# Relaying the y and z sums per batch on TensorE instead of by DMA copies, in an attention and spectral-mix kernel

## The chip, the cores and the metric

The kernel runs on one core of a Trainium2 chip. The core has five engines, each with its own in-order instruction stream: TensorE (PE in the profile; its weight loads are the row PEld), VectorE (DVE), ScalarE (ACT), GpSimd (POOL) and SyncE (SP, which here issues only transfers). Sixteen DMA engines move data; they are shared by every queue, whichever engine issued the transfer. The metric is the device time of one execution in microseconds (us). Over three runs the kernel before takes 439.65 us in the median (439.11 to 439.7).

## The reference

```python
def phi(x):
    proj = np.einsum('bhsd,df->bhsf', x, w_phi)
    proj = proj - np.max(np.abs(proj), axis=-1, keepdims=True)
    return np.concatenate([np.exp(proj), np.exp(-proj)], axis=-1)
q_p, k_p = (phi(q), phi(k))                    # q, k, v: 8 x 8 x 576 x 64
kv = np.einsum('bhsf,bhsd->bhfd', k_p, v)
z = np.sum(k_p, axis=2)
num = np.einsum('bhsf,bhfd->bhsd', q_p, kv)
den = np.einsum('bhsf,bhf->bhs', q_p, z)[..., None] + 1e-06
x = (num / den), heads side by side             # 8 x 576 x 512
X = np.fft.rfft(x, axis=1)                      # 64 modes are kept
Yr = Xr @ w_r - Xi @ w_i ;  Yi = Xr @ w_i + Xi @ w_r   # w_r, w_i: 64 x 512 x 512, one matrix per mode
y = np.fft.irfft(Y, n=S, axis=1)
u = x + y
return u + np.maximum(u @ w_ch, 0.0)            # w_ch: 512 x 512
```

Inputs and output are float32. The two weight tensors are 67 MB each in float32 and have to be read once.

## The kernel before

**Attention.** The first loop (line 503) runs over 16 units: four groups g of two heads by four pairs bp of batches. Iteration n works on up to four units at different stages: it turns k and q of one, exponentiates and multiplies with v for the next, and takes the finished unit through `freq`, a small matmul with a cosine and sine table that gives its 64 modes. The result x stays in SBUF as `xs`; the modes go to `XT`. Loads of q, k and v are issued by POOL (`load_k`, `load_q`, `load_v`), with a cast to bf16 for q and k; `vn` has two buffers, so the load for unit n + 2 is issued once `weigh_v2` of unit n has read its buffer (the two `va` multiplies on DVE).

**Weights and mix steps.** A mix step (`mix`, line 461) multiplies one load of weights with the modes: 8 modes (one value of o, 0 to 7), one group g of 128 input channels, the real or the imaginary tensor (i = 0 or 1). There are 64 of them, and each needs one load of 1 MB in bf16 (2 MB read as float32 by POOL's queue, which casts). The weights lie in nine rotating buffers of the pool `pw`, tag `wt`; a load waits until the mix step that read its buffer has run, and `next_w(1)` stands after each mix step in the program. The queue is first in, first out. I number the mix steps 0 to 63 in the order in which they run; `some(n)` runs them inside the attention loop, up to number 43, three of these in its last iteration (n = 16). The steps 44 to 63 run in the loop `while mixq` (line 923). The order of the last 20 is: group 3, o = 0 to 5, real and imaginary (44 to 55), then o = 6 and o = 7, each with group 2 real, group 2 imaginary, group 3 real, group 3 imaginary (56 to 63). When the second of a pair of group 3 is done (i = 1), the sums y of these 8 modes are complete: `yst` is 128 rows (8 modes by real and imaginary by 8 batches) of 512.

**What is made of y.** For each o the code adds `yacc` (`yst`, DVE), turns it with four transposes (`yT`), multiplies it with w_ch (8 matmuls, `pz`) into `zst`, and so has y and z = y @ w_ch of these modes. Rows of one o hold all 8 batches, but the inverse transform needs, for one batch, the modes of all o under each other. For that `put` (line 816) sends `yst` and `zst` by DMA from SP into `yall` and `zall`, 128 KB each, in the layout [mode rows, batch, 512]. The rows of o = 6 and 7 go also, as extra copies, into `yl`, four transfers from POOL (o = 6) and four from SP (o = 7).

**Products.** x consists of 36 chunks of 128 tokens by 512: (bp, n) with n = 0 to 8. `Channels.turn` and `product` turn a chunk and multiply it with w_ch: 4 transposes and 4 matmuls, copied by ACT into `xw`. Three chunks (the last of 36, K = 33) are not copied: `hold` leaves their product in PSUM and the z part is added there later.

**Sums.** `Absorb` adds to each chunk the inverse transform of o = 0 to 5 (of o = 0 to 6 for the eight chunks with bp = 0, n < 8, called early): one matmul with `yall` into p (`sum_p`), one with `zall` into q (`sum_q`). DVE adds p to x in `xs` (`keep_x`); ACT copies q into `xw` (`keep_w`). So that the old `xw` is in the sum, a third matmul with the identity adds it first, except for 14 chunks marked `aside`: there ACT copies q into a spare float32 tile and POOL adds `xw`. The order is fixed by the list `todo`: products first, then the sums, taken off by `fill(n)` between the mix steps, with n worked out from what is left.

**PSUM.** In this phase there are eight banks: four single ones (`bank`, tile `pt`) and two double ones (`banks`, tile `pp`). `all` takes alternately two single banks and one double one for p and q.

**Output.** After mix step 63 the part of o = 7 is still missing (o = 6 and 7 for the chunks that aren't early). Lines 984 to 1022 (class `Last`) add it from `yl` or straight from `yst` and `zst`, apply the maximum, add, and store from SP in 20 transfers. The change leaves this part as it is.

Of the kernel before, what the change touches and what calls it, by code (L numbers as in the profile page):

```python
# [19 lines left out]
NG = 4  # L21
# [22 lines left out]
def kernel(  # L44
# [455 lines left out]
    def unit(i):  # L500
        return units[i] if 0 <= i < len(units) else None

    for n in range(-2, len(units) + 1):
        P, Q, K, R = (unit(n + i) for i in (-1, 0, 1, 2))
        X = 0 if n < 4 else 6 if n == 4 else 3
        if Q:
# [4 lines left out]
        if Q:  # L511
            Q.weigh_v2()
            if unit(n + 2):
                unit(n + 2).load_v()
        if P:
# [47 lines left out]
        if Q:  # L563
            Q.num(12)
        some(X - 2 + (n == 12))
        if n == -1:
# [15 lines left out]
    def bank(shape=(128, DMODEL), dt=F32):  # L582
        return pst.tile(list(shape), dt, name="pt", tag="pt")
# [5 lines left out]
    pb = pb_cm.__enter__()  # L589
    xw = pb.tile([128, NP, 9, DMODEL], BF16, name="xw", bufs=1)  # L590
    zall = pw.tile([128, B_, DMODEL], BF16, name="zall", tag="wt")
    yall = pw.tile([128, B_, DMODEL], BF16, name="yall", tag="wt")
# [86 lines left out]
    class Channels:  # L679
# [28 lines left out]

        def hold(self, pf):
            for g in range(NG):  # L710
                pe.matmul(pf, lhsT=self.xT[:, g, :], rhs=wchb[:, g, :],
                          start=(g == 0), stop=False)

    def back(p, c, bp, table, src, r, stop=True, start=False):
# [9 lines left out]
    class Absorb:  # L724
# [34 lines left out]

        def only_x(self):  # L760
            self.sum_p(bank())
            self.keep_x()

        def only_w(self):
            back(self.q, self.n, self.bp, self.table, zall, self.rows)
            self.keep_w()

        def all(self):
            if full.index(self) % 2:
                p, q = bank(), bank()  # L770
            else:
                t = banks()
                p, q = t[:, 0], t[:, 1]
            self.sum_p(p)
            self.sum_q(q)
            self.keep_x()
            self.keep_w()
# [4 lines left out]
    ab = [Absorb(*c) for c in chunks]  # L782
    K = len(ch) - 3
    full = sorted(ab[:K], key=lambda c: c.early)
    spare = []
    for c in full[0:28:2]:
        c.aside = True

    tables = inverse_tables()

    def hold(i):
        next(tables, None)
        if i + 1 < len(ch):
            ch[i + 1].turn()
        if i < K:
            ch[i].product()
            if chunks[i] in stored:
                ch[i].back_x()
            return
        if i == K:  # L800
            t = banks()
            ab[i].q, ab[i + 1].q = t[:, 0], t[:, 1]
        elif i == K + 2:
            ab[i].q = bank()
        ch[i].hold(ab[i].q)

    todo = [ch[0].turn] + [lambda i=i: hold(i) for i in range(len(ch))]
    todo += [c.only_x for c in ab[K:]] + [c.only_w for c in ab[K:]] + [c.all for c in full]
    A = 3 * 3 + K

# [4 lines left out]

    def put(src, o, dst, copies):
        if o < 7:
            sp.dma_start(dst[16 * o:16 * o + 16], src)
        if o > 5:
            for s in copies:  # L820
                r = 32 * s + 16 * (o - 6)
                (pool if o == 6 else sp).dma_start(yl[r:r + 16], src)

# [99 lines left out]
    while mixq:  # L923
# [10 lines left out]
        mix(*key, wts.pop(key), XTb[g % 2], bank)  # L934
        next_w(1)
        left = len(mixq)
        if left > 8:
            n = -(-max(len(todo) - A - 2, 0) // (left - 8))
        elif left == 8:
            n = 2  # L940
        else:
            n = math.ceil(len(todo) / max(left - 0.6, 0.4)) if left else 0
        if g == NG - 1 and i == 1:
# [3 lines left out]
            pt = [bank([128, 2, 128], BF16) for h in range(2)]  # L947
            yT = [pb.tile([128, 2, 128], BF16, name=f"yT{h}") for h in range(2)]
            for h in range(2):
                dve.tensor_tensor(out=yst[:, H * h:H * h + H], in0=py[:, H * h:H * h + H],  # L950
                                  in1=yacc[:, o, H * h:H * h + H], op=ALU.add)
            put(yst, o, yall, (0, 2))
            if o < 5:
                fill(min(n, 1))
            for h in range(2):
                for dc in range(2):
                    pe.transpose(pt[h][:, dc, :],
                                 yst[:, H * h + 128 * dc:H * h + 128 * dc + 128], ident_b)
                if h:
                    dve.tensor_copy(yT[h], pt[h])  # L960
                else:
                    act.copy(yT[h], pt[h])
            if o < 5:
                fill(min(n - 1, 1))
            elif end:
                seq[0].straight(0)
                seq[0].keep_p()
                seq[2].straight(0, (0,))
            cut = (slice(0, 384), slice(384, DMODEL))
            pz = [bank([128, e.stop - e.start]) for e in cut]  # L970
# [8 lines left out]
            dve.tensor_copy(zst[:, cut[1]], pz[1])  # L979
            put(zst, o, zall, (1, 3))  # L980
            fill(max(n - 2, 0) if o < 5 else n)
        else:
# [71 lines left out]
```

## Time and profile before

| what | us |
|---|---|
| median of three runs | 439.65 |
| the profiled execution's own time | 440.25 |
| its span, first to last instruction | 438.5 |
| PE busy, share of the span | 332.0 (76%) |
| DVE busy | 296.4 (68%) |
| ACT busy | 279.4 (64%) |
| POOL busy | 113.0 (26%) |

The profiled execution is 0.60 us slower than the median, and 1.75 us of its time lie outside the span. The page gives the busy time of each engine over the whole span; stages with different limits are averaged in it, so a stage has to be read with the windows and the timeline, which give the same figures for one stretch. Almost every instruction passes through one recording helper, so the profile shows line 37 for all of them, and groups are told apart by the tiles that they write and read: `pt<-wt,XT` is a mix step, `pt<-ident_b,xs` are a chunk's transposes, `pt<-wchb,xT` its product, `xs<-pp,xs` is `keep_x` from a double bank, `rl<-pp` the copy of an `aside` sum. The duration of a matmul in the timeline includes its way through the array, so that successive ones overlap: what one costs in a row of them is the distance from start to start.

### The profile page before, as it was taken

The page shows a single profiled execution, that of the slowest core. Times are in us where ns is not written, and L with a number is a line of the kernel's source. Part 1 is how long each engine was busy: PE and PEld are TensorE (multiplying, and loading weights), DVE is VectorE, ACT ScalarE, POOL GpSimd, SP SyncE. Part 2 cuts the span into 40 slices and gives each one's busy share as a digit, 9 for nine tenths or more (in the row PEclk, how much of TensorE's full clock was granted, in tenths as well). Part 3 has the DMA queues.
Part 4 walks back from the last instruction along what each step waited for, and adds up shares of the span by engine and source line. Part 5 has one row for each costly group of instructions (what it writes and reads, how often), then busy time and mean ns, then how long its engine had stood idle before and what let it go on. Part 6 is the DMA issues. An engine that isn't in the chain of part 4 may idle for free.

```text
span 438.5 us, 10107 instructions
## 1 busy us (share of the span) xinstructions
PE 332.0 (76%) x4190; PEld 202.1 (46%) x4233; DVE 296.4 (68%) x583; ACT 279.4 (64%) x478; POOL 113.0 (26%) x151
## 2 busy tenths in 40 slices
PE   2687678688687687687787787284789999998993
PEld 1355456465465465455465555152444554333320
DVE  5667776765786877976986888243784333886684
ACT  3786786776986886875875876210553442665781
POOL 6232132113221222221222221121101111483072
PEclk9998796789998999996996998876899999999996
DMA  9999999999999999999999999999999999996787
GB/s 213 209 212 210 237 212 237 237 212 248 228 211 239 225 228 232 237 215 235 232 217 239 210 239 211 238 213 212 212 215 223 219 222 224 212 219 135 242 361 309
DMA packets 51710, 99.55 MB, mean 227 GB/s; under 512 B 2512, under 2 KB 13648, under 8 KB 51664
## 3 DMA queue, kind: packets, MB, share of 16 engines
q0 software_dynamic: 45232, 85.86, 99.7%
q1 hardware_dynamic: 6272, 12.98, 8.5%
q8 instruction: 33, 0.54, 0.5%
q14 instruction: 13, 0.11, 0.1%
q10 hardware_dynamic: 160, 0.07, 0.1%
HBM read 163.64 MB, written 9.44 MB: 395 GB/s over the span
## 4 chain that ended last, share of the span: by engine, by line
PE 43%; DVE 22%; ACT 18%; DMA 10%; issue 5%; POOL 0%; POOLq 0%; ACTq 0%; DVEq 0%
PE pt L37 17%; PE one L37 14%; DMA wt<-in_moe_w_r_dram 8%; PE two L37 8%; ACT AB L37 7%; DVE m L37 6%; DVE mk L37 6%; PE pp L37 4%; ACT AQ L37 3%; ACT XT L37 3%; DVE xs L37 2%; DVE XT L37 2%; DMA qb<-in_q_dram 2%; ACT qT L37 1%; DVE yacc L37 1%
## 5 line engine op out<-in xcount | busy, mean ns | idle before, releaser
L37 ACT ACTIVATE AB<-two 128x1024 bf16<-128x1024 f32 x64 | 62.0, 1024 | 10.6 <-DVE mk L37 7.2
L37 ACT ACTIVATE AQ<-two 128x1024 bf16<-128x1024 f32 x64 | 62.6, 1043 | 2.0 <-PE two L37 1.8
L37 ACT CAST xw<-pt 128x512 bf16<-128x512 f32 x50 | 29.4, 588 | 41.9 <-PE pt L37 41.8
L37 DVE TENSOR_REDUCE m<-two 128x8 f32<-128x1024 f32 x32 | 39.2, 1224 | 15.8 <-PE two L37 15.7
L37 DVE TENSOR_TENSOR va<-vn,ee 128x1152 bf16<-128x1152 f32 x32 | 42.0, 1355 | 8.2 <-DMA vn<-in_v_dram 8.2
L37 DVE TENSOR_REDUCE mk<-two 128x8 f32<-128x1024 f32 x32 | 38.9, 1218 | 7.7 <-PE two L37 7.7
L37 POOL DMA_DIRECT2D wt<-in_moe_w_i_dram x28 | 21.0, 750 | 86.4 <-PE pt L37 37.7
L37 POOL DMA_DIRECT2D wt<-in_moe_w_r_dram x30 | 22.5, 751 | 69.2 <-PE one L37 30.7
L37 PE MATMUL pt<-wchb,xT 128*128 128x512 bf16 x127 | 35.6, 393 | 5.2 <-DVE xT L37 3.5
L37 PEld LDWEIGHTS <-xs 128*128 128x128 bf16 x624 | 31.6, 103 | 12.6 <-issue 7.3
L37 PE MATMUL two<-w2blk,qT 128*128 128x256 bf16 x128 | 22.1, 301 | 20.2 <-ACT AB L37 8.4
L37 ACT COPY qT<-one 128x512 bf16<-128x512 bf16 (+1 forms) x32 | 19.3, 641 | 27.5 <-PE one L37 27.2
L37 PEld LDWEIGHTS <-qT 128*128 128x128 bf16 x144 | 14.6, 103 | 36.8 <-issue 33.2
L37 PE MATMUL one<-wt,XT 128*32 128x512 bf16 x304 | 27.5, 452 | 4.9 <-DMA wt<-in_moe_w_i_dram 3.3
L37 PE MATMUL two<-mT,minus 96*128 96x512 bf16 x64 | 28.5, 446 | 3.2 <-issue 1.5
L37 PEld LDWEIGHTS <-AQ 128*128 128x128 bf16 x512 | 25.8, 111 | 8.8 <-issue 5.6
L37 PE MATMUL one<-kvz,AQ 128*128 128x65 bf16 x512 | 28.4, 212 | 1.2 <-ACT qT L37 0.8
L37 DVE COPY xT<-pt 128x512 bf16<-128x512 bf16 x36 | 17.0, 472 | 17.8 <-PE pt L37 17.8
L37 PE MATMUL one<-va,AB 64*128 64x65 bf16 x1024 | 22.5, 199 | 8.3 <-DVE va L37 8.3
L37 DVE RECIPROCAL rd<-one 128x6 f32<-128x6 f32 x48 | 9.4, 196 | 27.6 <-PE one L37 27.5
L37 DVE TENSOR_TENSOR xs<-one,rd 128x384 bf16<-128x384 f32 x48 | 26.7, 557 | 1.6
L37 POOL DMA_DIRECT2D kb<-in_k_dram x16 | 11.4, 714 | 62.2 <-PE one L37 57.2
(151 smaller groups left out, 719.3 us busy)
## 6 DMA issues: line engine op xcount, KB each, us to landing
wt<-in_moe_w_r_dram POOLq DMA_DIRECT2D x30, 1024.0 KB, 28.1
wt<-in_moe_w_i_dram POOLq DMA_DIRECT2D x28, 1024.0 KB, 28.4
out_dram<-of SPq DMA_DIRECT2D x16, 512.0 KB, 4.0
vn<-in_v_dram POOLq DMA_DIRECT2D x14, 576.0 KB, 24.6
kb<-in_k_dram POOLq DMA_DIRECT2D x16, 288.0 KB, 20.4
qb<-in_q_dram POOLq DMA_DIRECT2D x16, 288.0 KB, 18.3
xs<-in_moe_w_i_dram POOLq DMA_DIRECT2D x2, 1024.0 KB, 23.1
vn<-in_v_dram SPq DMA_DIRECT2D x2, 576.0 KB, 4.6
```

What stands on the lines that cost most here:

```text
L37: ins = f(*args, **kwargs)
```

## The change

Seven things change in the phase behind the attention, and two in the attention loop.

- y of o = 0 to 5 is not sent to `yall` and `zall` by DMA any more, and z is not worked out per o. Instead the turned y goes into a new tile `yTa`, [128 channels, 4, batch, o, 16], straight from the transposes' PSUM (two copies per o, by ACT and DVE, with rearranged axes). The tile takes one of the nine weight buffers.
- A new function `relay(b)` makes one batch of `yall` and `zall`: four transposes of `yTa` back into a bank, four matmuls of it with w_ch into a second bank, one copy by DVE (y) and one by ACT (z). There are eight, one per batch. For batches 0 and 1 also o = 6 is in it, which two small DVE copies from `yT` bring into `yTa`.
- o = 6 and 7 keep their own z (8 matmuls) and the copies to `yl`; `put` issues these alone.
- All 36 chunks get a product in `xw` and a sum by `all`; `hold`, `only_x` and `only_w` are gone. The sums are ordered by descending bp.
- `two_banks` hands out the double bank twice and then two single ones, in turn, to sums and relays.
- The list `todo` ends in relay 6, a product, relay 7, the last product, and then the 36 sums with the other six relays between them. All of this stands behind mix step 56.
- `next_w(1)` is left out after three mix steps, as one weight buffer fewer is to be had.
- The attention loop's last iteration runs no mix steps: steps 41 to 43 move into the loop `while mixq`, behind the first products.
- The last unit's v is loaded from SP's queue instead of POOL's.

```diff
@@ -1,4 +1,5 @@
 
+import itertools
 import math
 from contextlib import ExitStack
 
@@ -502,7 +503,7 @@
 
     for n in range(-2, len(units) + 1):
         P, Q, K, R = (unit(n + i) for i in (-1, 0, 1, 2))
-        X = 0 if n < 4 else 6 if n == 4 else 3
+        X = 0 if n < 4 or n == len(units) else 6 if n == 4 else 3
         if Q:
             Q.exp_q(0)
         if K:
@@ -511,7 +512,7 @@
         if Q:
             Q.weigh_v2()
             if unit(n + 2):
-                unit(n + 2).load_v()
+                unit(n + 2).load_v(sp if n + 2 == len(units) - 1 else pool)
         if P:
             P.freq()
             assert not any(key[0] == P.g - 2 for key in mixq)
@@ -562,7 +563,7 @@
                 unit(n + 4).load_q()
         if Q:
             Q.num(12)
-        some(X - 2 + (n == 12))
+        some(X - 2 + (n == 12) if X else 0)
         if n == -1:
             forward_table()
         if n < 3:
@@ -588,6 +589,7 @@
     pb_cm = tc.tile_pool(name="pb", bufs=2)
     pb = pb_cm.__enter__()
     xw = pb.tile([128, NP, 9, DMODEL], BF16, name="xw", bufs=1)
+    yTa = pw.tile([128, 4, B_, 7, 16], BF16, name="yTa", tag="wt")
     zall = pw.tile([128, B_, DMODEL], BF16, name="zall", tag="wt")
     yall = pw.tile([128, B_, DMODEL], BF16, name="yall", tag="wt")
     yl = pw.tile([128, B_, DMODEL], BF16, name="yl", tag="wt")
@@ -706,11 +708,6 @@
                           start=(g == 0), stop=(g == 3))
             act.copy(xw[:, self.bp, self.n, :], pf)
 
-        def hold(self, pf):
-            for g in range(NG):
-                pe.matmul(pf, lhsT=self.xT[:, g, :], rhs=wchb[:, g, :],
-                          start=(g == 0), stop=False)
-
     def back(p, c, bp, table, src, r, stop=True, start=False):
 
         if c < 8:
@@ -757,20 +754,8 @@
             else:
                 act.copy(w, self.q)
 
-        def only_x(self):
-            self.sum_p(bank())
-            self.keep_x()
-
-        def only_w(self):
-            back(self.q, self.n, self.bp, self.table, zall, self.rows)
-            self.keep_w()
-
         def all(self):
-            if full.index(self) % 2:
-                p, q = bank(), bank()
-            else:
-                t = banks()
-                p, q = t[:, 0], t[:, 1]
+            p, q = two_banks()
             self.sum_p(p)
             self.sum_q(q)
             self.keep_x()
@@ -780,46 +765,60 @@
     chunks.sort(key=lambda c: c not in stored)
     ch = [Channels(*c) for c in chunks]
     ab = [Absorb(*c) for c in chunks]
-    K = len(ch) - 3
-    full = sorted(ab[:K], key=lambda c: c.early)
+    full = sorted(ab, key=lambda c: -c.bp)
     spare = []
     for c in full[0:28:2]:
         c.aside = True
+    turn = itertools.cycle((0, 0, 1))
+
+    def two_banks():
+        if next(turn):
+            return bank(), bank()
+        t = banks()
+        return t[:, 0], t[:, 1]
+
+    def relay(b):
+
+        at = slice(0, 6 + (b < 2))
+        n = 16 * at.stop
+        cols = [yTa[:, dc, b, at].rearrange("p o k -> p (o k)") for dc in range(4)]
+        py, pz = two_banks()
+        py = py.bitcast(BF16)[:, 0:512]
+        for dc in range(4):
+            pe.transpose(py[:n, 128 * dc:128 * dc + 128], cols[dc], ident_b)
+        for dc in range(4):
+            pe.matmul(pz[:n], lhsT=cols[dc], rhs=wchb[:, dc, :],
+                      start=(dc == 0), stop=(dc == 3))
+        dve.tensor_copy(yall[:n, b], py[:n])
+        act.copy(zall[:n, b], pz[:n])
 
     tables = inverse_tables()
 
-    def hold(i):
+    def product(i):
         next(tables, None)
         if i + 1 < len(ch):
             ch[i + 1].turn()
-        if i < K:
-            ch[i].product()
-            if chunks[i] in stored:
-                ch[i].back_x()
-            return
-        if i == K:
-            t = banks()
-            ab[i].q, ab[i + 1].q = t[:, 0], t[:, 1]
-        elif i == K + 2:
-            ab[i].q = bank()
-        ch[i].hold(ab[i].q)
-
-    todo = [ch[0].turn] + [lambda i=i: hold(i) for i in range(len(ch))]
-    todo += [c.only_x for c in ab[K:]] + [c.only_w for c in ab[K:]] + [c.all for c in full]
-    A = 3 * 3 + K
+        ch[i].product()
+        if chunks[i] in stored:
+            ch[i].back_x()
+
+    todo = [ch[0].turn] + [lambda i=i: product(i) for i in range(len(ch))]
+    tail = [c.all for c in full]
+    for at, b in ((24, 1), (22, 0), (17, 3), (14, 2), (7, 5), (5, 4)):
+        tail.insert(at, lambda b=b: relay(b))
+    tail = [lambda: relay(6), todo[-2], lambda: relay(7), todo[-1]] + tail
+    A = len(tail)
+    todo[-2:] = tail
 
     def fill(n):
         for _ in range(n):
             if todo:
                 todo.pop(0)()
 
-    def put(src, o, dst, copies):
-        if o < 7:
-            sp.dma_start(dst[16 * o:16 * o + 16], src)
-        if o > 5:
-            for s in copies:
-                r = 32 * s + 16 * (o - 6)
-                (pool if o == 6 else sp).dma_start(yl[r:r + 16], src)
+    def put(src, o, copies):
+        for s in copies:
+            r = 32 * s + 16 * (o - 6)
+            (pool if o == 6 else sp).dma_start(yl[r:r + 16], src)
 
 
     class Last:
@@ -932,8 +931,9 @@
             for c in (seq[0], seq[2]):
                 c.base(0)
         mix(*key, wts.pop(key), XTb[g % 2], bank)
-        next_w(1)
         left = len(mixq)
+        if left not in (19, 9, 8):
+            next_w(1)
         if left > 8:
             n = -(-max(len(todo) - A - 2, 0) // (left - 8))
         elif left == 8:
@@ -945,27 +945,39 @@
             py = pys.pop(o)
             yst = pb.tile([128, DMODEL], BF16, name="yst")
             pt = [bank([128, 2, 128], BF16) for h in range(2)]
-            yT = [pb.tile([128, 2, 128], BF16, name=f"yT{h}") for h in range(2)]
+            yT = [pb.tile([128, 2, 128], BF16, name=f"yT{h}") if o > 5 else None
+                  for h in range(2)]
             for h in range(2):
                 dve.tensor_tensor(out=yst[:, H * h:H * h + H], in0=py[:, H * h:H * h + H],
                                   in1=yacc[:, o, H * h:H * h + H], op=ALU.add)
-            put(yst, o, yall, (0, 2))
-            if o < 5:
+            if o > 5:
+                put(yst, o, (0, 2))
+            if not end:
                 fill(min(n, 1))
             for h in range(2):
                 for dc in range(2):
                     pe.transpose(pt[h][:, dc, :],
                                  yst[:, H * h + 128 * dc:H * h + 128 * dc + 128], ident_b)
+                src = pt[h].rearrange("p c (k b) -> p c b k", b=B_)
+                into = yTa[:, 2 * h:2 * h + 2, :, o] if o < 6 else None
                 if h:
-                    dve.tensor_copy(yT[h], pt[h])
+                    dve.tensor_copy(*((into, src) if o < 6 else (yT[h], pt[h])))
                 else:
-                    act.copy(yT[h], pt[h])
-            if o < 5:
-                fill(min(n - 1, 1))
-            elif end:
+                    act.copy(*((into, src) if o < 6 else (yT[h], pt[h])))
+            if o < 6:
+                fill(n - 1)
+                continue
+            if o == 6:
+                for h in range(2):
+                    dve.tensor_copy(
+                        yTa[:, 2 * h:2 * h + 2, 0:2, 6],
+                        yT[h].rearrange("p c (k b) -> p c b k", b=B_)[:, :, 0:2])
+            if end:
                 seq[0].straight(0)
                 seq[0].keep_p()
                 seq[2].straight(0, (0,))
+            else:
+                fill(1)
             cut = (slice(0, 384), slice(384, DMODEL))
             pz = [bank([128, e.stop - e.start]) for e in cut]
             for e in range(2):
@@ -977,8 +989,8 @@
             zst = pb.tile([128, DMODEL], BF16, name="zst")
             act.copy(zst[:, cut[0]], pz[0])
             dve.tensor_copy(zst[:, cut[1]], pz[1])
-            put(zst, o, zall, (1, 3))
-            fill(max(n - 2, 0) if o < 5 else n)
+            put(zst, o, (1, 3))
+            fill(n - 2)
         else:
             fill(n)
     assert not todo
```

## The prediction

> **What bounds the kernel now.** I read the page's slices first, then the queues in two stretches, then the timeline of PE behind the attention. The slices say that the DMA engines are full until some 40 us before the end:
>
> ```profile
> DMA  9999999999999999999999999999999999996787
> GB/s 213 209 212 210 237 212 237 237 212 248 228 211 239 225 228 232 237 215 235 232 217 239 210 239 211 238 213 212 212 215 223 219 222 224 212 219 135 242 361 309
> ```
>
> The transfers between 280 and 320 us, and then those between 320 and 400 us, show what the copies into `yall` and `zall` cost the stream of weights:
>
> ```profile
> q0 software_dynamic: 4241, 8.45, 111.7%
> ```
>
> ```profile
> q0 software_dynamic: 7790, 15.54, 102.3%
> q1 hardware_dynamic: 2016, 1.84, 8.6%
> ```
>
> POOL's queue (q0) moves 8.45 MB in 40 us alone, but 15.54 MB in 80 us beside the 14 copies of SP's queue (q1, 1.84 MB): 1.36 MB less than twice 8.45, so 6.4 us of stream. Undisturbed, a load of 1.05 MB takes 1.05 / (8.45 / 40) = 4.96 us.
>
> The timeline of PE shows who waits. Steps 43 and 44 wait for weights; the later ones don't. The others are prices:
>
> ```profile
> 297.11 0.66 PE L37 MATMUL one<-wt,XT 128*32 128x512 bf16 x8 [3.30 <-DMA wt<-in_moe_w_i_dram]
> 302.11 1.08 PE L37 MATMUL pt<-wt,XT 128*32 128x512 bf16 x8 [4.34 <-DMA wt<-in_moe_w_r_dram]
> ...
> 351.07 0.66 PE L37 MATMUL pt<-wt,XT 128*32 128x512 bf16 x8
> 351.66 0.40 PE L37 MATMUL pt<-ident_b,xs 128*128 128x128 bf16 x4
> 351.89 1.03 PE L37 MATMUL pt<-wchb,xT 128*128 128x512 bf16 x4
> 352.76 0.39 PE L37 MATMUL pt<-ident_b,xs 128*128 128x128 bf16 x4
> ...
> 368.50 0.66 PE L37 MATMUL pt<-wt,XT 128*32 128x512 bf16 x8
> ...
> 403.11 0.66 PE L37 MATMUL pt<-wt,XT 128*32 128x512 bf16 x8
> ```
>
> From start to start a mix step costs 0.59 us, four transposes 0.23, four matmuls over 512 columns 0.87 (0.217 each). Step 56 starts at 368.50, step 63 at 403.11. The windows between, and from there to the end:
>
> ```profile
> 368.50:403.11 34.61, 32.23 (x192) 12.52 (x193) 25.08 (x42) 21.24 (x39) 19.03 (x19) 1.00 1.04 207
> 403.11:438.50 35.39, 27.62 (x157) 9.24 (x157) 23.12 (x24) 20.16 (x38) 11.38 (x10) 0.90 0.76 283
> ```
>
> PE is busy for 32.2 of 34.6 us (first figure after the length): here PE with the copies behind it is the bound, and the weights are just ahead. The end follows step 63 by 35.39 us of output work.
>
> **The change, part by part.** *Copies gone.* All 14 leave SP's queue and the stream keeps 4.96 us a load. Step 44's weights landed at 302.1; step 56 is twelve loads on, 302.1 + 12 x 4.96 = 361.6; step 63's land at 302.1 + 19 x 4.96 = 396.3. So step 56 may start 368.50 - 361.6 = 6.9 us earlier. The loads' own issue doesn't spoil it: they take 25 to 42 us from issue to landing, five to eight loads deep, and with `yTa` in one buffer a load still waits for the step eight before its own (the last one six before, some 26 us ahead of 396). POOL issues it behind two additions of 1.16 us; the four `yl` transfers of o = 6 follow it on POOL, as now.
>
> *The last v, and three steps moved.* This row is the last unit's v:
>
> ```profile
> 282.33 2.63 DVE L37 TENSOR_TENSOR va<-vn,ee 128x1152 bf16<-128x1152 f32 x2 [8.21 <-DMA vn<-in_v_dram]
> ```
>
> On SP it leaves as soon as its buffer is free (the `va` row of two units before ends at 246.9) and isn't behind five loads. Price on SP: 4.6 us alone at the start, 6.5 for a copy in the full stream, against 24.6 on POOL; any of them is before 274, where DVE wants it. The 8.2 us fall away, but the bytes are the same, and what is late next is the weights of step 41, due at 302.1 - 3 x 4.96 = 287.2. There the products start, 15 us earlier than now. The tables on DVE come along (steps 44 to 48 take 30 us with them, DVE busy 25.6 us of 300 to 340) and end near 317; then a step with two products costs 0.59 + 2 x 1.10 + 0.23 = 3.0 us against 4.96 a load, so PE has caught up with the loads by step 51, at 337, five loads before step 56. Steps 51 to 56 then wait for weights. The two y copies per o (between 0.29 us, `yT`, and 0.73, the `xT` copy with rearranged axes) lie in these waits of 1.9 us; z per o (8 matmuls, 0.87) leaves a stretch that waits anyway, worth nothing. If that cover were gone, 12 x 0.44 = 5 us at most would be DVE's and ACT's, half each.
>
> *Behind step 56.* Relays need o = 5, so they all stand here. PE's content from step 56 to 63, before: 7 steps 4.1, 36 sums (y and z, 0.43 each; the four in halves 0.48) 15.7, 19 identity matmuls 4.1, products and held ones 3.1, o = 6 1.1, the output's first five 1.1: 29.2. The actual 34.61 thus holds 5.4 us of waits. After: the eight relays add 8 x (0.23 + 0.87) = 8.8, three more identities 0.65, the products fall to 2.0: 29.2 + 8.8 + 0.65 - 1.1 = 37.55. The weights for step 63 allow 396.3 - 361.6 = 34.7, so PE remains the bound, not the stream. DVE gets 8 copies more (0.42, the `xT` row), ACT 8 (0.59) and 3: 28 each, of about 42 us.
>
> *The waits.* Removed: at o = 6 PE waited 1.1 us for `yst` and `yT`; now a relay stands between. Step 56, now with 0.9 us of waits, is filled with products and relays, and three sums no longer come in two pieces, where steps 57 and 58 lose 1.2: I count 2.8 us less in all. Added: a double bank is taken again after three users instead of four. These rows tell how long one is held, 388.79 to 390.82:
>
> ```profile
> 388.79 0.39 PE L37 MATMUL pp<-yall,CI 96*128 96x512 bf16 x1
> 389.02 0.38 PE L37 MATMUL pp<-zall,CI 96*128 96x512 bf16 x1
> 389.44 0.69 DVE L37 TENSOR_TENSOR xs<-pp,xs 128x512 bf16<-128x512 f32 x1
> 390.22 0.60 ACT L37 COPY rl<-pp 128x512 f32<-128x512 f32 x1 [0.40 <-DVE xs L37]
> ```
>
> ACT reads only after DVE: 2.0 us, 2.2 with an identity, 2.4 for a relay. Three users give PE 1.5 to 2.3 us of work. Going through the order, six reuses come 0.2 to 0.5 too early, 1.7 in all. PE is in order: what waits for a bank holds back the mix step behind it. Waits after: 5.4 - 2.8 + 1.7 = 4.3. Bounds: 1.5 (six steps with 0.13 us, as the best one now, and the 0.75 for ACT before step 63) and 7.5 (waits in today's share, 5.4 / 29.2 x 37.55 = 6.9, and a third of the reuses). I take 4.3, near the middle and from its own terms.
>
> *Sum.* Step 63 at 361.6 + 37.55 + 4.3 = 403.45, against 403.11. Output unchanged, 35.39: span 438.84, +0.34 us, so 440.59 for the profiled execution, and on the median **440.0**, no change. The stream's 6.9 us are spent on 8.35 us of more PE work, less 1.1 of waits.
>
> *Two rules weighed.* The row has four transposes in 0.23 us. The Trainium skill (TensorE: Matmul & The Clock Gate, Part 4: PE-mode transpose) gives about 275 ns for one in a kernel, which speaks against this change: 32 in the relays would be an estimated 8.8 us instead of 1.8, and the end 447. The row decides.
>
> The clock is the second. Two stretches (the third figure from the end is the granted clock):
>
> ```profile
> 45.60:49.00 3.40, 1.51 (x50) 1.24 (x43) 2.81 (x4) 3.19 (x5) 0.45 (x1) 1.00 1.12 211
> 49.00:52.40 3.40, 2.37 (x17) 1.85 (x17) 2.26 (x7) 2.36 (x9) 0.00 (x0) 0.50 1.12 243
> ```
>
> With PE busy 1.51 of 3.40 us the next stretch runs at half clock. PE's waits of 1.9 us in 4.96 put some stretches near that edge, and 3.4 us at half clock at step 56 would cost 1.7 us. The same page (What's actually happening) asks for a whole idle window of about 3.4 us before the clock falls, which would make it nothing. I take nothing, and put 1.7 in the range.
>
> **Rivals.** *Faster: the relays fill the waits.* For: DVE, at 0.60 us a sum and 25 of 34.6 us, sets the pace of PE's 0.43 to 0.65 now, and relays give it air. Against: the held banks. With waits of 2.0 us step 63 comes at 401.15, the median 437.7.
>
> *Slower: the double banks.* Two of three users now go through two double banks. If one is held 0.4 us longer than above, because DVE or ACT is still at another bank, the early reuses grow from six to about fifteen: 3 us more, 443.0. It decides from 0.1 us of longer holding (0.7 us in all). For: ACT waits for DVE in the row above. Against: relays between sums spread the users out.
>
> *The end belongs to the stream*: PE's work fits into 34.7 us, step 63 at 396.3, median 432.8. Against: 37.55 us are counted.
>
> *The copies cost nothing*, and the stream stays at (8.45 x 2 / 15.54) x 4.96 = 5.39 a load: step 56 at 366.8 as now (its weights), step 63 at 408.65, median 445.2. Against: the two queue rows.
>
> **How the numbers follow.** No change 0.36, relays fill the waits 0.30, double banks or the clock 0.29, stream 0.03, copies 0.02. Of the first, 0.26 lie inside 0.2% (0.9 us, about what a measurement tells from no change), 0.05 on either side: faster 0.38, same 0.26, slower 0.36. The range from the bounds of the waits: 361.6 + 37.55 + 1.5 gives 437.2, waits of 7.5 give 443.2; both rivals of any weight lie in it. The stream as the bound lies outside, so I take 0.6 us more below: 436.6 to 443.2.
>
> **What would show it.** Right: no `yall<-yst` in SP's queue, q0 at 8.45 MB per 40 us up to 396, PE waiting for weights before steps 51 to 56, step 56 near 361.6, 0.22 us between a relay's matmuls, step 63 not waiting for weights, 35.4 us behind it. Wrong: step 56 later than 363 (stream, or PE not caught up), many waits of `pp` matmuls for ACT's copies, half clock near 361, or step 63 waiting for its weights.

## The result, and the profile after

The changed kernel takes **440.29 us** (median of 14 runs, 440.06 to 440.87) against 439.66 us for the kernel before (14 runs, 438.97 to 440.19): a ratio of 1.0018, 95% interval 1.0010 to 1.0026. That is 0.63 us more, inside the 0.9 us that I took for no change, and 0.3 us above the 440.0 predicted. The profiled execution took 440.27 us with a span of 438.5 us, the same span as before (its own time there was 440.25 us).

Equal spans hide a large exchange. The page's slices of the DMA engines first (busy share in tenths, then GB/s):

```profile
DMA  9999999999999999999999999999999999990788
GB/s 217 209 212 210 238 213 236 238 212 249 227 211 238 227 229 228 237 216 233 233 216 238 233 239 212 212 212 212 212 212 212 212 212 212 212 204 27 239 339 333
```

The stream of weights now runs at 212 GB/s without a dip from slice 25 on, and is over at the end of slice 36, half a slice earlier than in the page of before. POOL's queue between 320 and 360 us, with no copies beside it:

```profile
q0 software_dynamic: 4248, 8.44, 112.0%
```

8.44 MB in 40 us, the undisturbed 8.45 of the prediction. The timeline of PE: its rows for the mix steps around the end of that stage (those between them left out), and the first two relays.

```profile
336.37 0.66 PE L38 MATMUL pt<-wt,XT 128*32 128x512 bf16 x8 [1.05 <-DMA wt<-in_moe_w_i_dram]
341.38 0.66 PE L38 MATMUL pt<-wt,XT 128*32 128x512 bf16 x8 [1.46 <-DMA wt<-in_moe_w_r_dram]
346.31 0.66 PE L38 MATMUL pt<-wt,XT 128*32 128x512 bf16 x8 [1.99 <-DMA wt<-in_moe_w_i_dram]
351.23 0.66 PE L38 MATMUL pt<-wt,XT 128*32 128x512 bf16 x8 [0.24 <-DMA wt<-in_moe_w_r_dram]
356.18 0.66 PE L38 MATMUL pt<-wt,XT 128*32 128x512 bf16 x8 [2.00 <-DMA wt<-in_moe_w_i_dram]
361.20 0.66 PE L38 MATMUL pt<-wt,XT 128*32 128x512 bf16 x8 [1.47 <-DMA wt<-in_moe_w_r_dram]
361.79 0.42 PE L38 MATMUL pp<-ident_b,yTa 128*96 128x128 bf16 x4
362.05 1.03 PE L38 MATMUL pp<-wchb,yTa 128*96 128x512 bf16 x4
...
364.00 0.39 PE L38 MATMUL pp<-ident_b,yTa 128*96 128x128 bf16 x4
364.22 1.03 PE L38 MATMUL pp<-wchb,yTa 128*96 128x512 bf16 x4
```

The first six rows are steps 51 to 56, 4.9 to 5.0 us apart, all waiting for their load: step 56 now starts at 361.20 instead of 368.50. A relay's transposes take 0.22 to 0.26 us from start to start. Two windows, step 56 to step 63 and step 63 to the end (busy time of PE, PEld, DVE, ACT and POOL, then PE's clock, the DMA share and GB/s):

```profile
361.20:403.88 42.68, 40.72 (x248) 17.92 (x251) 29.73 (x51) 26.14 (x48) 19.06 (x19) 1.00 0.88 171
403.88:438.50 34.62, 27.70 (x157) 9.23 (x157) 23.13 (x24) 20.16 (x38) 11.36 (x10) 0.92 0.78 288
```

So the change gains 7.30 us ahead of step 56, gives 8.07 us back between steps 56 and 63 (42.68 against 34.61), and the output is 0.77 us shorter with the same 157 matmuls. In these three numbers lies the whole case. The waits in the first of the two windows that concern double tiles (engine, what, for whom: total us, times, longest):

```profile
ACT zall L38 <- DVE yall L38: 8.8, 8, 3.2
ACT xw L38 <- DVE xs L38: 5.0, 9, 0.9
...
ACT rl L38 <- DVE xs L38: 2.2, 4, 0.9
...
PE pp L38 <- ACT xw L38: 0.9, 3, 0.4
...
PE pp L38 <- ACT rl L38: 0.2, 1, 0.2
```

The upper three rows are ScalarE's: for a double tile (`pp`) it starts only when VectorE is done with the other half. In the timeline all 21 of these reads are of `pp`, none of a single bank. The lower two are what the view shows PE to lose by that, 1.1 us; the experiments show that it loses more.

### The profile page after: what moved, and what is told of

It reads as the page before. It is cut to its first block, busy times and chain, and to the rows that moved or that the text cites. A ratio compares the mean times of both kernels' runs of the same rounds, so it can differ in the third digit from the quotient of the medians.

```text
span 438.5 us, 10103 instructions
## 1 busy us (share of the span) xinstructions
PE 333.7 (76%) x4208; PEld 203.0 (46%) x4252; DVE 300.9 (69%) x587; ACT 282.3 (64%) x483; POOL 111.9 (26%) x150
## 4 chain that ended last, share of the span: by engine, by line
DMA 39%; PE 26%; DVE 16%; ACT 11%; issue 5%; POOL 1%; POOLq 0%; ACTq 0%; DVEq 0%
DMA wt<-in_moe_w_r_dram 22%; DMA vn<-in_v_dram 12%; PE pt L38 9%; PE one L38 7%; PE pp L38 6%; DMA qb<-in_q_dram 5%; PE two L38 4%; ACT AB L38 4%; DVE m L38 3%; DVE mk L38 3%; ACT AQ L38 2%; DVE xs L38 2%; ACT xw L38 1%; DVE xw L38 1%; ACT XT L38 1%
## 5 line engine op out<-in xcount | busy, mean ns | idle before, releaser
L38 ACT CAST xw<-pt 128x512 bf16<-128x512 f32 x45 | 26.4, 586 | 46.2 <-PE pt L38 46.2
L38 PE MATMUL pt<-wchb,xT 128*128 128x512 bf16 x135 | 40.0, 410 | 7.6 <-DVE xT L38 5.8
L38 PE MATMUL two<-mT,minus 96*128 96x512 bf16 x64 | 27.1, 424 | 3.3 <-issue 1.5
L38 PEld LDWEIGHTS <-XT 128*32 128x32 bf16 x512 | 14.5, 149 | 31.5 <-issue 19.6
L38 PE MATMUL one<-wt,XT 128*32 128x512 bf16 x288 | 25.6, 442 | 3.9 <-DMA wt<-in_moe_w_i_dram 2.3
L38 PE MATMUL two<-w2blk,kT 128*128 128x256 bf16 x128 | 20.7, 289 | 8.7 <-ACT AB L38 8.7
```

Of the source, the lines that this page charges most:

```text
L38: ins = f(*args, **kwargs)
```

## The experiments

My theory: between steps 56 and 63 TensorE's content is the bound, with some waits for double tiles in it; ahead of step 56 it is the stream of weights. Rivals: the double tiles' pace is itself the bound; the stream didn't need the copies' removal; the early v or the moved steps carry the gain. All kernels are variants of the changed one unless said otherwise. Step 56 is read from each timeline and the 56-to-63 time is from step to step.

**The copies, put back** (`copies_back`).

```diff
+    scratch = pb.tile([128, 4, DMODEL], BF16, name="scratch", bufs=1)
...
             if o < 6:
+                for s in range(2):
+                    sp.dma_start(scratch[:, 2 * (o % 2) + s], yst)
                 fill(n - 1)
                 continue
```

> The changed kernel with 12 copies of 128 KB of y on SyncE's queue again (two per o below 6), into a scratch tile that nobody reads. Theory (copies on SyncE's queue take their share of the weights' stream: 6.4 us for 14 of them): 12/14 x 6.4 = 5.5 us, nearly all of it ahead of step 56; step 56 starts at 366 to 367 instead of 361.2, and the end follows: 444.5 to 446. Rival (the copies lie in gaps of the queue): step 56 within 1 us of 361.2 and the time within 0.3% of 440.3.

Measured 445.66 us, 5.4 us above the changed kernel (ratio to before 1.0144, interval 1.0123 to 1.0165). The two queues between 320 and 360 us:

```profile
q0 software_dynamic: 3797, 7.54, 99.7%
q1 hardware_dynamic: 1419, 1.29, 12.1%
```

While 1.29 MB of copies passed, the stream lost 0.90 MB of 8.44, 4.3 us at 0.211 MB per us. Step 56 starts at 365.51, 4.3 us later, a little short of the 366 to 367 expected, and its weight load on PE waits for the DMA:

```profile
365.51 0.21 PEld L38 LDWEIGHTS <-XT 128*32 128x32 bf16 x8 [0.60 <-DMA wt<-in_moe_w_r_dram]
```

The 56-to-63 time is 42.69 us, as in the changed kernel. The copies do cost stream time, and in this kernel stream time is the kernel's time. The profiled execution took 445.20 us, 4.9 more than that of the changed kernel: 4.3 of it lie ahead of step 56 and 0.6 in the output.

**The copies alone taken out of the kernel before.** A first form (`before_no_copies`) kept the copies of o = 0 only, and let the sums read just these 16 rows.

```diff
-            self.rows = slice(0, 112 if self.early else 96)
+            self.rows = slice(0, 16)
...
-        if o < 7:
+        if o < 1:
             sp.dma_start(dst[16 * o:16 * o + 16], src)
```

> The kernel before with the copies of o = 0 alone; the inverse sums read 16 rows only, so the part of the output that comes from the modes of o = 1 to 6 is left out. Theory (TensorE, late by the 8.2 us wait for the last v, is what sets step 56 there, with the weights just ahead of it): the stream gains 5 to 6 us, but TensorE comes to step 56 at most 1 us earlier: 438.6 to 439.9. Rival (the copies alone were the bound): step 56 some 5 us earlier and a time near 434.

Measured 463.55 us (ratio 1.0544), which neither theory had. Step 56 answers the question (367.76, 0.74 us earlier); behind it TensorE ran at half clock. The second form (`before_fill`) keeps the rows of the sums and drops all the copies into `yall` and `zall`; GpSimd fills these once.

```diff
-        if o < 7:
-            sp.dma_start(dst[16 * o:16 * o + 16], src)
...
+            if o == 4:
+                pool.memset(yall, 0.5)
+                pool.memset(zall, 0.5)
```

> The kernel before without any of the copies into the two tiles that the inverse sums read; GpSimd fills them with a constant once, so the part of the output that comes from the modes of o = 0 to 6 is left out, and the sums keep their 96 and 112 rows. Theory (late by the wait for the last v, TensorE sets step 56 in the kernel before; the copies alone aren't its bound): step 56 at 367.5 to 368.5, the time 438.4 to 440.0; and the half clock behind step 58 in the run with 16 rows came from the 16 rows. Rival for that: the clock falls again, and the time is 450 or more.

Measured 439.41 us, ratio 0.9990 (0.9978 to 1.0003): no difference that can be told. Step 56 starts at 367.26, only 1.2 us earlier, and without a wait for weights:

```profile
367.26 0.66 PE L37 MATMUL pt<-wt,XT 128*32 128x512 bf16 x8
```

The same stretch of both, first with 16 rows, then with 96 and 112:

```profile
378.00:388.00 10.00, 10.00 (x29) 2.10 (x29) 4.79 (x8) 4.64 (x8) 4.05 (x4) 0.50 1.12 212
```

```profile
378.00:388.00 10.00, 9.28 (x54) 3.50 (x52) 8.13 (x15) 6.68 (x13) 8.13 (x10) 1.00 1.12 212
```

So in the kernel before, TensorE itself arrived late at step 56, and the removal of copies gave nothing there; in the changed kernel the same removal is worth 5.4 us. The copies' removal pays only together with other parts of the change. The half clock is taken up at the end.

**The last v, and the three steps.** First v alone goes back to GpSimd's queue (`v_pool`), then also steps 41 to 43 go back into the attention loop (`loop_back`).

```diff
-                unit(n + 2).load_v(sp if n + 2 == len(units) - 1 else pool)
+                unit(n + 2).load_v()
```

> The last unit's v goes back from SyncE's queue to GpSimd's, behind the weight loads; everything else stays. Theory (the stretch before step 56 has 9 to 10 us in which TensorE only waits for weights, so lateness before it is made up): the attention part ends up to 8 us later, TensorE catches up later than step 51, step 56 starts between 0 and 1.0 us later, and the time is 440.3 to 441.3. Rival (the early v is what pays for the relays): 445 us or more.

Measured 440.33 us, against 440.29. The wait for v is back, and the timeline shows it made up before step 56 (VectorE's `va` row; then the rows of steps 54 to 56 on PE):

```profile
281.69 2.63 DVE L38 TENSOR_TENSOR va<-vn,ee 128x1152 bf16<-128x1152 f32 x2 [9.28 <-DMA vn<-in_v_dram]
```

```profile
350.92 0.66 PE L38 MATMUL pt<-wt,XT 128*32 128x512 bf16 x8 [0.36 <-DMA wt<-in_moe_w_r_dram]
355.87 0.66 PE L38 MATMUL pt<-wt,XT 128*32 128x512 bf16 x8 [2.02 <-DMA wt<-in_moe_w_i_dram]
360.88 0.66 PE L38 MATMUL pt<-wt,XT 128*32 128x512 bf16 x8 [1.46 <-DMA wt<-in_moe_w_r_dram]
```

PE catches up at step 54 instead of 51, and that is enough. The early v is worth nothing here.

```diff
-        X = 0 if n < 4 or n == len(units) else 6 if n == 4 else 3
+        X = 0 if n < 4 else 6 if n == 4 else 3
...
-        some(X - 2 + (n == 12) if X else 0)
+        some(X - 2 + (n == 12))
```

> The last unit's v on GpSimd's queue and the three weight steps 41 to 43 back inside the last round of the attention loop, as in the kernel before; the copies stay away. Theory: with the copies gone the weights of step 56 land at 361.2 us in any case and TensorE has caught up before, so 440.0 to 441.3. Rival (the moved steps are a part of the balance): 443 us or more.

Measured 440.94 us (440.58 to 441.83), 0.65 above the changed kernel. Steps 54 to 56 start at 355.22, 359.18 and 362.65 without any wait for weights: here PE doesn't quite catch up, and step 56 is 1.45 us late in the profiled execution, which at 441.82 us is one of the longest. In the median the moved steps are worth 0.6 us, within what was expected.

Compared with `before_fill`, which also has no copies, a late v and its steps in the loop, step 56 is 4.6 us earlier (362.65 against 367.26). What left TensorE there is z per o, 6 x 0.87 = 5.2 us; I didn't isolate it (the held chunks differ too), but it is the largest difference between the two. Nor was the kernel before tried with the early v alone.

**How soon a double tile comes round.** In the changed kernel two of three sums or relays use a double tile. Now every second one (`alt_banks`), or every one (`all_double`).

```diff
-    turn = itertools.cycle((0, 0, 1))
+    turn = itertools.cycle((0, 1))
```

> The two banks of a sum or relay come from the double tiles every second time instead of every third (the other time from single banks). The theory that the content of TensorE sets the stretch from step 56 to step 63, with 5.1 us of waits in it of which some 1.7 are the double tiles coming round too early (held 2.0 to 2.4 us, three users between two of the same tile): with two users between them these come round sooner or later by one user, so the time changes by less than 1.7 us either way; central guess +0.5 us (440.8). The rival that the double tiles aren't waited for at all: no change beyond 0.2%.

Measured **437.98 us**, ratio to before 0.9959 (0.9944 to 0.9973), 2.3 us below the changed kernel. The expectation left the sign open, guessed the wrong one, and allowed for less than 1.7 us.

```diff
-    turn = itertools.cycle((0, 0, 1))
+    turn = itertools.cycle((0,))
```

> All sums and relays take both banks from the double tiles, so that one comes round after two users. Theory (a double tile is held 2.0 to 2.4 us, because ScalarE reads its half only after VectorE, and TensorE waits in order for it): two tiles give one sum per 1.0 to 1.2 us against 0.65 us of matmuls; over 36 sums that is some 14 us more, of which the mix steps, products and o = 6 (8 us) take a part: step 63 4 to 7 us later, 444 to 447. Rival (every second time was better for another reason, such as the order of the engines' work): within 1 us of 440.3.

Measured 452.32 us, 12 us above it. The window from step 56 to step 63, with tiles reused after four users (`alt_banks`) and after two (`all_double`); the changed kernel's 42.68 above is with three:

```profile
361.34:401.65 40.31, 39.87 (x248) 17.86 (x252) 27.90 (x51) 26.28 (x49) 19.07 (x19) 1.00 0.93 180
```

```profile
361.15:415.83 54.68, 44.19 (x252) 18.28 (x253) 30.98 (x51) 27.81 (x49) 19.05 (x19) 1.00 0.69 134
```

PE issues the same matmuls in all three (248, 248 and 252 records, as a few are missing). With four users it is busy for 39.87 of 40.31 us. Busy time can hide short waits, though: the same matmuls count as 44.19 us with two users. The waits in `all_double` for tile halves:

```profile
ACT xw L38 <- DVE xs L38: 11.5, 20, 0.9
...
PE pp L38 <- ACT xw L38: 5.3, 13, 0.6
PE pp L38 <- ACT zall L38: 2.9, 6, 0.7
...
PE pp L38 <- ACT rl L38: 1.7, 4, 0.7
```

PE's own waits for a tile grow from 1.1 us at 4 places to 9.9 us at 23. The expectation of 4 to 7 us was too small; I had let mix steps and products run beside these waits, but PE is in order, and they stand behind them.

**z left out of the relays**, with the changed kernel's banks (`no_z`) and then with those of `alt_banks` (`no_z_alt`; its expectation stands below).

```diff
-        for dc in range(4):
-            pe.matmul(pz[:n], lhsT=cols[dc], rhs=wchb[:, dc, :],
-                      start=(dc == 0), stop=(dc == 3))
         dve.tensor_copy(yall[:n, b], py[:n])
-        act.copy(zall[:n, b], pz[:n])
+        act.copy(zall[:n, b], py[:n])
```

> The relays leave out their four z matmuls; the second copy reads y's bank again, so the z of o below 6 is left out. Theory (TensorE's content behind step 56 is the bound): 8 x 0.87 = 7.0 us leave it; step 63's weights land at 395.8, so step 63 starts at 396 to 399, and the time falls by 4.5 to 7 us, to 433.3 to 435.8. Rival (double tiles and the engines that empty them set the pace): the waits grow by most of what leaves, and the time falls by less than 2.5 us.

Measured 437.87 us, only 2.4 below the changed kernel: the rival's number, but not quite its mechanism. The 56-to-63 time falls by 3.79 us (to 38.89) where 7.0 us of matmuls left, so 3.2 us, not most of the 7.0, came back as waits; step 56 came 0.76 us later in this execution, and the last stores 1.1 us later (below).

> The relays without their z matmuls (the z of o below 6 is left out of the output), and banks from the double tiles every second time. Theory (without z the double tiles' pace took over as the bound behind step 56; without both it is the stream): content 37.55 - 7.0 = 30.6 and waits of some 2.8 bring TensorE to step 63 at 395, its weights land at 395.8 to 397, so step 63 waits for them and the time is 396.5 + 34.6 to 35.7 + 1.75 = 432.9 to 434. Rival (VectorE's or ScalarE's work is the next bound): step 63 without a wait for weights, 435.5 or more.

Measured 433.83 us, ratio 0.9867 (0.9849 to 0.9884). The 56-to-63 time is 35.00 us; the weights of step 63 had landed at 396.70 (issued at 369.09, 27.6 us on the way), and it starts at 396.74. The timeline shows no wait there, so stream and TensorE arrive together; the expectation of a visible wait was wrong, its time right. Without z the banks are worth 4.0 us, with it 2.3: less content uncovers more of the tile's pace. Content and tiles both bind in the changed kernel, and neither alone is the bound.

**A better kernel.** z is made turned, per o, in the stretch that waits for weights (`turned_z`); six of the eight relays then turn it with four transposes. (A small table of VectorE gets 8 columns fewer to make room.)

```diff
+    zTa = pb.tile([128, 4, 6, 6, 16], BF16, name="zTa", bufs=1)
...
-        for dc in range(4):
-            pe.matmul(pz[:n], lhsT=cols[dc], rhs=wchb[:, dc, :],
-                      start=(dc == 0), stop=(dc == 3))
+        if b > 1:
+            pz = pz.bitcast(BF16)[:, 0:512]
+            for e in range(4):
+                pe.transpose(pz[:n, 128 * e:128 * e + 128],
+                             zTa[:, e, b - 2].rearrange("p o k -> p (o k)"), ident_b)
+        else:
+            for dc in range(4):
+                pe.matmul(pz[:n], lhsT=cols[dc], rhs=wchb[:, dc, :],
+                          start=(dc == 0), stop=(dc == 3))
...
             if o < 6:
                 fill(n - 1)
+                zt = bank([128, 4, 6, 16])
+                for e in range(4):
+                    for dc in range(4):
+                        pe.matmul(zt[:, e].rearrange("p b k -> p (b k)"),
+                                  lhsT=wchb[:, dc, 128 * e:128 * e + 128],
+                                  rhs=yTa[:, dc, 2:8, o],
+                                  start=(dc == 0), stop=(dc == 3))
+                dve.tensor_copy(zTa[:, :, :, o], zt)
                 continue
```

> z is made turned as well, per step of o below 6, by 16 small matmuls into one bank and one copy, in the stretch that waits for weights; the relays of six of the eight batches then turn it with four transposes (0.23 us) in place of four matmuls (0.87 us). Theory (TensorE's content behind step 56 sets the end): 6 x 0.64 = 3.8 us leave that content, step 63 starts near 400.0 instead of 403.9, and the time falls by 2.5 to 3.9 us to 436.4 to 437.8, less what the new matmuls (some 8 us in 10 us of idle time before step 56) push step 56 back. Rival 1 (the waits between ScalarE, VectorE and TensorE behind step 56 set the end): the waits grow and the time stays within 0.3%. Rival 2 (the stretch before step 56 has no room): step 56 starts 3 us or more later and the time is 440 or more.

Measured 439.52 us, 0.8 below the changed kernel, short of the 436.4 to 437.8 expected and equal to before (0.9994, 0.9983 to 1.0004). The 56-to-63 time falls by 2.38 of the 3.8 us; step 56 is 0.9 us later, and the last stores land 1.1 us later behind step 63. With the alternation added (`turned_alt`):

> z turned in the stretch that waits for weights, and banks from the double tiles every second time. Theory (behind step 56 it is TensorE's content of 37.55 us plus waits for banks; the two edits take from different terms): turned z alone took 2.4 us from the stretch between steps 56 and 63 and gave 0.9 back ahead of it, the alternation took 2.4; together 440.3 - 2.3 - 0.8 = 437.2, or 436.0 if the waits that turned z left for banks go too. Rival (both remove the same waits): no better than the alternation alone, 438.0.

Measured 436.68 us (0.9930, 0.9918 to 0.9943), half a microsecond better than the first figure expected. At last four more sums add their chunk on GpSimd (`turned_alt_aside`):

```diff
-    for c in full[0:28:2]:
+    for c in full[0:35:2]:
         c.aside = True
```

> z turned ahead, banks from the double tiles every second time, and 18 instead of 14 sums add their chunk on GpSimd, so that four identity matmuls (0.22 us each) leave TensorE. Theory (TensorE's content is still the bound between steps 56 and 63): 0.9 us less, 435.8 to 436.3. Rival (GpSimd, at 1.4 us an addition, or the waits take it back): 436.6 or more.

Measured **435.84 us**, ratio to before **0.9913** (0.9898 to 0.9928): 3.8 us faster than before, 4.5 faster than the change. Its window:

```profile
361.20:398.18 36.98, 36.32 (x247) 16.08 (x246) 27.49 (x51) 25.40 (x48) 23.15 (x23) 1.00 1.02 198
```

POOL's busy time rose by 4 us, at no cost that shows. The weights of step 63 landed at 396.38 (issued at 369.38, 27.0 us on the way), so at most 1.8 us are left before the stream is the bound.

## Why the prediction was right, and where a term was not

*Copies gone, step 56 at 361.6.* Right: 361.20, and the stream at 8.44 MB in 40 us. With the copies put back the time is 445.66, close to the 445.2 of the rival in which the stream stays slow.

*The last v and the three steps.* PE catching up by step 51 near 337 was right (336.37, and 1.05 us of waiting). But the case didn't need it: with the late v it catches up by step 54, and the time is the same. In the changed kernel the late v's wait, 9.3 us in `v_pool`, has no price; what the 8.2 us cost in the kernel before no run shows.

*z per o "worth nothing".* Right for the changed kernel, where that stretch waits anyway; `loop_back` beside `before_fill` suggests that it is worth more than the early v as soon as PE is late.

*Content 37.55 plus waits 4.3.* The sum was 41.85 and came to 42.68. The term that was mis-sized is the reuse of double tiles: 1.7 us in the prediction, 2.4 by `alt_banks` (42.68 against 40.31). The tiles were held about as long as I had said: in the timeline of the changed kernel, in the median, 2.0 us without an identity, 2.2 with one and 2.3 for a relay. But more of them come back too early. Of 28 reuses, 9 start within 0.1 us of the end of ScalarE's read, where I had counted six. One of them, a relay that waits for its tile:

```profile
390.46 0.58 ACT L38 CAST zall<-pp 112x512 bf16<-112x512 f32 x1 [0.96 <-DVE yall L38]
...
391.10 0.38 PE L38 MATMUL pp<-ident_b,yTa 128*112 128x128 bf16 x4
```

In `alt_banks` no reuse starts within 0.4 us of the release; in `all_double` 31 of 42 start within 0.1 us. The rival of longer held tiles happened at one place: the relay at o = 6 held its tile for 3.9 us, behind a slow copy of VectorE (last section). Between steps 59 and 60, where this lies, `alt_banks` gains 0.8 of its 2.4 us (6.97 against 7.79), so up to that much of the 2.4 may not be early reuse alone.

The rest of the waits measures 40.31 - 37.55 = 2.8, against 5.4 - 2.8 = 2.6 predicted. In `alt_banks` the view shows no wait of PE's matmuls for another engine. A part of this rest is time between matmuls of changing kinds, which I had left out of the content, such as 0.31 us from a sum to a mix step where 0.22 is the usual distance:

```profile
374.64 0.38 PE L38 MATMUL pt<-zall,CD 96*128 96x512 bf16 x1
374.95 0.66 PE L38 MATMUL pt<-wt,XT 128*32 128x512 bf16 x8
```

*Faster rival, 437.7: "the relays fill the waits".* It didn't happen by itself, since the banks were against it, as the prediction said. With the banks alternating the time is 437.98.

*Stream as the bound, 432.8.* Not the case with z in the relays; reached by `no_z_alt` (433.83).

*Output 35.39.* It was 34.62, with the same matmuls behind step 63. The last store leaves 31.1 us after step 63 before and 31.0 after, but lands at 34.1 before and 33.5 after. The stores of that stage, median from issue to landing from 430 us on, before and then after:

```profile
out_dram<-of SPq DMA_DIRECT2D x2, 512.0 KB, 3.9
out_dram<-ofr SPq DMA_DIRECT2D x2, 256.0 KB, 3.3
```

```profile
out_dram<-of SPq DMA_DIRECT2D x3, 512.0 KB, 3.2
out_dram<-ofr SPq DMA_DIRECT2D x2, 256.0 KB, 2.8
```

The sum took 35.39 from the one profiled execution of before, which was 0.60 us above its median; where in it these 0.60 us lie no run shows. The term was 0.77 us too long and the waits 0.83 too short, so the two nearly cancelled, step 56 came 0.4 earlier, and the span came out at 438.5 against 438.84. That the median was met within 0.3 us is partly luck; the mechanism, and its sizes within a microsecond each, were right. The chunks no longer held were not tried alone.

*The two rules.* The transpose price of about 275 ns (the Trainium skill, TensorE: Matmul & The Clock Gate, Part 4: PE-mode transpose) didn't show: four took 0.22 to 0.26 us in a row. As for the clock, one window near step 53 has PE busy for 1.46 of 3.41 us and the next runs at half clock, so no whole idle window was needed:

```profile
344.36:347.77 3.41, 1.46 (x15) 0.77 (x16) 0.74 (x3) 0.58 (x1) 0.48 (x1) 1.00 1.12 211
347.77:351.18 3.41, 3.00 (x13) 1.46 (x12) 1.19 (x4) 0.95 (x3) 0.26 (x1) 0.50 1.12 212
```

It lies between steps 53 and 54 and was paid out of the waits for weights; behind step 56 the clock stayed full, as taken.

## What to carry to other kernels

Taking traffic off a stream pays only where the engine that uses the stream is on time: much the same copies were worth nothing measurable in one kernel and 5.4 us in the other, so look at who waits at the point where both meet. When work is moved behind that point, count how many users lie between two uses of the same buffer as well as the engine's content: one number in the rotation of the banks moved this kernel by 2.3 us one way and 12 the other. A wait at the front that the profile shows in full (9.3 us in `v_pool`) costs nothing if a later stretch waits for something else anyway.

## What the runs showed of the hardware that was not expected

TensorE's clock fell to half, and stayed there, with TensorE busy. In `before_no_copies` the sums read 16 rows instead of 96 or 112; from 375.3 us on the clock is at 0.50 for 51 us, with PE busy for 2.65 of the 3.30 us before that and for 10.00 of 10 us in the stretch shown above, and one matmul of a sum takes 0.43 us from start to start instead of 0.23:

```profile
374.69 0.38 PE L37 MATMUL pp<-yall,CD 16*128 16x512 bf16 x1
374.92 0.37 PE L37 MATMUL pp<-zall,CD 16*128 16x512 bf16 x1
...
376.45 0.63 PE L37 MATMUL pp<-yall,CD 16*128 16x512 bf16 x1
376.88 0.63 PE L37 MATMUL pp<-zall,CD 16*128 16x512 bf16 x1
```

`before_fill`, with the same order of matmuls over 96 and 112 rows, stays at 1.00. The two also differ in the data that the sums read (copies of o = 0 there, a constant here), so the rows are the likely cause and not the only difference. The kernel before points the same way: in its output, where many matmuls read 32 rows of `yl`, a window with PE busy for 2.68 of 3.42 us is followed by half clock:

```profile
427.85:431.27 3.42, 2.68 (x16) 0.84 (x13) 2.81 (x4) 2.17 (x4) 2.59 (x3) 1.00 1.01 393
431.27:434.68 3.41, 1.12 (x2) 0.12 (x2) 2.25 (x3) 0.00 (x0) 0.00 (x0) 0.51 1.00 389
```

No run isolates the rows. The Trainium skill (TensorE: Matmul & The Clock Gate, Part 1: The HAM clock gate) ties the clock to how busy PE is; here a PE that the profile shows as fully busy was not enough.

The last stores have two ways of landing. In the changed kernel, `alt_banks`, `v_pool`, `loop_back`, `copies_back` and `all_double` the last one lands 33.5 to 33.8 us after step 63; in the kernel before, `before_fill` and all kernels with z turned or left out it is 34.1 to 34.6, with the last store issued at 30.6 to 31.4 in all of them. It took about a microsecond off the gain of the kernels with z turned. Why wasn't settled.

A small copy of VectorE, from `yT` into `yTa` at o = 6, took 1.40 us beside an addition of GpSimd in the changed kernel (the first row holds two such copies). In `alt_banks` (second pair of rows) they were done before that addition began, at 0.22 us each:

```profile
383.33 1.53 DVE L38 COPY yTa<-yT 128x64 bf16<-128x64 bf16 x2 [0.79 <-ACT yT L38]
383.48 1.17 POOL L38 TENSOR_TENSOR xw<-rl,xw 128x512 bf16<-128x512 f32 x1
...
382.45 0.34 DVE L38 COPY yTa<-yT 128x64 bf16<-128x64 bf16 x2
383.45 1.17 POOL L38 TENSOR_TENSOR xw<-rl,xw 128x512 bf16<-128x512 f32 x1
```

It goes by the rotation of the banks: in all seven traces of the changed kernel and its variants without the alternation the first copy takes 1.40 to 1.42 us and ends within 0.1 us of the end of the addition; in the four with it, 0.22. VectorE's additions from PSUM kept their 0.68 us beside GpSimd's.
